# Row maxima of two heads by one VectorE instruction over two PSUM banks, in an attention and feed-forward kernel

## The chip, the cores and the metric

The kernel runs on one core of a Trainium2 chip. The metric is the device time of one execution in microseconds. TensorE (PE, with its weight loads PEld) multiplies matrices, VectorE (DVE), ScalarE (ACT) and GpSimd (POOL) do the work between products, and SyncE (SP) issues nearly all DMAs from one queue. Every engine works through its own list of instructions in order and waits on semaphores for the others. PSUM, where products are accumulated, is used here in banks of 512 fp32 columns on 128 partitions.

## The reference

The reference is attention over four batches and eight heads, with 576 positions of 64 values, followed by two feed-forward layers over the 2304 tokens. The mask lets a position see its own block of 64 and all earlier blocks.

```python
scores = scale * np.matmul(q, k.transpose(0, 1, 3, 2))
mask = block_i >= block_j
scores = np.where(mask, scores, -1000000000.0)
scores = scores - np.max(scores, axis=-1, keepdims=True)
attn = np.exp(scores)
attn = attn / (np.sum(attn, axis=-1, keepdims=True) + 1e-09)
out = np.matmul(attn, v)
...
h = x @ w_in
g = h * np.tanh(sp)
x = g @ w_out
...
h = np.maximum(x @ w_in, 0.0)
return h * h @ w_out
```

`sp` is log(1 + exp(h)). The first `x` is the attention's output with the heads side by side, 2304 x 512; `w_in` is 512 x 2048 and `w_out` 2048 x 512 in both layers. All is fp32, so the scores, the attention's second product and the feed-forward products are made in fp16 pieces (a high and a low part of each factor, three products instead of one), or in fp32 in a few places.

## The kernel before

The work is cut into pieces of 384 tokens, six for each layer. Attention fills the input tile `x` of a first-layer piece, two heads at a time. Two functions do it.

- `attention_lo` (from L1035) takes the 192 earliest queries of a batch for two heads, 16 units in all, in fp32. Its inputs come by two DMAs: q and k packed as 128 x 640 (L1042, into slots named `qk` or `vs`, two instructions of 320 columns in the trace) and v (L1043, `pb`). L1054 makes the scores of both heads in one PSUM bank, L1055 adds the mask, L1059 and L1060 take maxima, L1061 makes the exponent's bias of them, ScalarE takes exponentials, L1067 and L1069 make reciprocals, L823 and L825 scale by them, L1077 to L1080 transpose on PE, and L1092 and L1093 make the second product.
- `attention_hi` takes the other 384 queries of a batch for two heads, 16 units, in split fp16. Each unit has three tiles of 128 queries: tiles 2 and 3 with 320 and 448 keys, and tile 4 with 576, of which the last 128 are made together with tile 2 and the first 448 by themselves. So a unit has three groups of scores (320 + 128, 448 and 448 columns): `scores` (L909, mask at L913) writes head 0 into one PSUM bank and head 1 into the other; the slot for both is called `ab`, and there is only one. `peak` (L922) takes the row maxima, one VectorE instruction for each head. In the first group two copies (recorded at L791 on ScalarE and L793 on VectorE) move the 128 columns of tile 4, one copy for each head, to the SBUF tile `tl`, whose maxima L975 takes. `low` (L927) makes the exponents' bias of the maxima, `expo` (L933) the exponentials on ScalarE, one for each head, `finish` (L943 to L954) the reciprocals and the scaled probabilities as a high part (L953 on ScalarE or L954 on VectorE) and a low part (L818 on VectorE, tile `pb`), which a DMA transposes. `second` (L1018) makes the product with v.

A group of scores therefore holds both banks until the last reader of each is done: the maxima, the copies and the exponentials.

The feed-forward products have several forms: L1352 with an activation at L1357 behind it (PSUM slot `hp`, first half of a layer), L1464 (second half, slot `acc`), and forms with seven products instead of eight, L1385 (first half) and L1503 (second half). Weights of the first layer come raw by L1139 (128 x 8190 bytes each) into `arena` or `pad`, and are made into two fp16 parts by VectorE: a cast (L1149, or on ScalarE) and a shift-and-or (L1150). Later passes read them back from DRAM, where they were spilled (`wspill`). Scaled inputs of a piece go through L1121 (ACT) and L818 (DVE, tile `g`).

Nothing in the code's loops sets the order of the work. Every step is put into a list of tasks by `sch.add`, with engine, cost, tiles read and written; `choose` and `copy` allow a task several engines. The string `PLAN` then gives a position and an engine for each task, and `planned` reads it:

```python
seq = [self.tasks[i + int.from_bytes(raw[2 * i:2 * i + 2], "little", signed=True)] for i in range(n)]
for i, t in enumerate(seq):
    name = ("PE", "ACT", "DVE", "POOL", "SP")[raw[2 * n + i]]
    t.start, t.fillers = float(i), None
    t.eng, t.dur, t.fn, t.lock = [o for o in t.opts if o[0] == name][0] if t.opts else t.first
```

So each engine's list is written out by hand of a table, and semaphores follow from the tiles. A task's `banks` says which of the two PSUM banks it reads, for a rule of the planner that keeps two engines out of one bank at a time. SP's queue takes DMAs in the order of the table too.

Of the kernel before, what the change touches and what calls it, by code (L numbers as in the profile page):

```python
# [68 lines left out]
def seg_len(tiles):  # L69
# [34 lines left out]
    ";%|0Ul6|_5RWHeL^qr0^BRJ(Jxlgw1vwDHvFT>G%pZ3K^dvpV9Ht20Klr@`msN5{uSoJwNZPpv4uUxHz<r%q77V1@UtNg21qxTcoxKdZ?3cX&wl~=IwRe2q`"
    "FS4q>T*2!La<^QD|1Oo;dJ?|6T?WaAaw#$BB30yZX(dm{bX}ki<JpCp1D3|<IQfxJKj;8?LE6bZSldEo>O}ojTg!O;T|0w>CuFStq7CFrovc4<Q|T>l$!Ge#"
    "*2TK}rG`w@Q940C)P7i4Q$EnUh|feUxm||o=Q;*oca}HsSY!EEn<MKLb(Xy<BlI2_qP68c^dGKY>Ye!W9q{u98g)aHf%xSOWdDLTqqT$d!nfB+Wuy86$Uj@|"
    "CE~fJ2k5$-b%*u8#NZNg;W6T{Pan}2vHJ$e0Ac&Jqud9sddfh32qfLD2jl>|d&pxT_L!{KR&oh`Ze|LIOdlDb*MpyX^g3-|dP{p*C%g4VEx@MLa=G@=m2$Oo"
    "*DbnC_SxQgNV{oQyt+Yq>U_!Jc}z3S0O`O<?Q|CV`^gq<t8=w2R^2Wa>NFW99mt+p`28lb;dAtCCS#?o_LBd}Tyo}GITN3@)PL~ujnYF}Xm1%uwiIDu6a7S9"
    "<*&o~2`C#v9{<2&nvNoVAIf}PA#ck-d0!@J8&FqSXMr7&cccZ#pRVKd4R$w?Ux~nIusxLhZ^~<?sZ5lQ^m!T2l^4xI`<6b7?Du(n9{pzMP%!zKJPPI>1Dh}F"
    "2gG%Zenv)?<Fu#sBORv0<Vj9?TOTL#uY=r_JdEwX+M)WO%(JyY%WI%_fc#gU(`q24KX+f$XXGifRi8v|F<Ee>Tx|02=5W0XX=~8^0qR;$PJUd5lIsu2BhrQQ"  # L110
    "9+G}kz9sl$lRipTEx^0|xw8%ruhjv1HNO2<`-A6pWYm3n7r30Jcj!RybhqBh?v~)brQAt{nT>aQfzKKG08wg$$7hnm`@!Yq+DU%Wp2YtSa<RX*lMBhUV{)^O"
    ")SKmYG~1vT>cya^vtFTZ>$Ti(qrKSGNM1#^Q)PjkPHh~?s&mEVTq7#z#YD1`oG0gl>QkhhZpNQA&AG(?9O};5c(5&3+mf|y<#at0UC-7$GP;#C*GAO0#?pt1"
    "IEXtpp>+f5PdRy#E5&&6bYfe`)u!?vEhW`JXCpkgl*~H?+4pKc?)BHxB%4pCQqw=gXCuKt6}f^MogyF4BnPamiMH0ZK-)TS&R{;*qMjbLzfyT$lR{gSx?WGq"
    "NL^T=A_&+H4{X!&GTJ-=+8-iUGl|Lrl4r}~y(84-dt|M>mwP#~#@;PuL2F;UcQ**?2lw;^XXVM!JBY1Nb)J&~+Xss-MD|TcI);p6$n8ay7+@YDL$=_pRb+a9"
    "BJvKXDzHna(PQm);xU~po~HBk4%w;Q&}|11*+EslN!~Tvz)gF0PjH^L)j`YuV1oI&#7?2=EwY<*67^s`o}54g*XrMPjdrDGt|oV8+V*f$C;3a;Qv>TFr#YyZ"
    "58u?{Qx|zaenI1Eaxr<>Le8gV=Tn{9%XgeLi)c?k=QG){9u{mxmYgH4<qPy(NyY9Cc50B5lhJsxj-_T*qDB^=?YC6lue2e49H|{_H#wWUtcSNhqu!own^QZ_"
    "Al`X;AB;6Z*OII6>%aOEIu6r|=o%Uj`)qdAk!Oi<8FUj6w-sx9V&zb3r4s+=K*n1AT`CfRhIlpyPp<&CkAZ=c$+Wuc{EseVZF_Xv&igj7XvnX>i2GP@b4<UH"
    "Hppm56)r=@ucDeC&`rmC>w82wm-^61-jzD!rotn0i0BsBvk3m~j`W)Nye7UWP1YZz+H|I(??r<Pq_RAX?SrtP5KrWj?`5cxkD%!W?Aed4v$SbYoebHfGw4<f"
    "`53^a4S2oXYyKhLIS6OXhw<0Iyz_WpK;F**5!>*6iX9f)en+SIuuQ37D@>n>2YSG%ztBCbq#mtO$ELsO74%dWakY>~9yMSSJXc5s8Vhpr@a=jkZ)x=0Ps9uL"
    "N)vF#biA_zdpA)d_S1>|q?enycz=UV(FNuZQGbb!?P6B$#(ys2%XA(5n-A(vmUB7dU+_Gcm><^)W<9!(=W!A%=ju1`O$VfvHv-~TYszGsVz@EHV^&I=Nm#rI"  # L120
    ">|~e``mKt|FoCh~>^S`sZv9ECm~!wzv3#mWBsAsBA^f{ZvP~T`p1L#G6iKE@(F1PPEVENq;;F#Q)BUndie<A@GY^^t_-2#Lqbr#MpB{uUH_2bJU$V?hdWK~("
    "gPOS$`Ku%_D`hV73eaq+Y?W)wG&;KP&|?Fd{(;ONVP|?B_-hr&%HzBl<j#2fzDuUDqmx-E+vO*DM)%2LnJxby_ct_Kjoi_?P1bXD8K>XJ{>73nf6$H8H*5Ix"
    "EzCQRbGDF8UsEgB%2c^W*UJW3g?4LXh0K(-eBLU1<wyAn8}`W*`je@!(L$`5f)BovTlo7ua;!))%m(a#8*Z2>Z|XcwU5AFhNkw?<Wte6@9dLiWNIyo$YjrSe"
    "dxdU6<MEvJly)auzNK=lm09R{RDPA$(Psrc$t!dRQ{`oHY7u&TCg<p<`1W72^;Y<JGHc$DyYwk+TrOK|A9P!R4U6P=YTyle2A#n5$o_{tJ?Rj7(u15!23|=9"
    "O^~y+hyE!)NNaskuF+On3*K#^6FFxxD_$TIm(pEd1~1H%N%R^`(En-fW$LN=3%>bWN@+(uU58+4GaUm@wbPSyl2q4o=y5)QDc+OA_Diy+wZ1Fg$QN`XHR!6F"
    "Yh4{JRp75zBt)xGRQm=he9Gml(=>~-KOkEh==*ZLJZ8tjEDzec)Qk^gf&Cg8ufRdowTY?D`UlMrWW6gL`5fqTbh;mi+A8$&Z_x3)EEVW(GUzPI(d`_x=fE1m"
    "3H$6SJ6K9%`IYd+Qri!fIb`qR%ANEVeO;eG&+)Dp-EE(d<8}bn6x-*e$kw3i&D1=5j6HewX*poG(QUUd1$KoUXfNaQT3d$B<VN|;mXiJUDLT5Fkd|jvZ<IUb"
    "B(vMjvo}b-onvnyGBblbyM=vy<WJdXH`*RxJkMsDN%nf)Q!r#VnQG5M&n`0EuC(9TE9G6Di)<(9DnGJnp&f_B#_|O#7u$|9#*ViOY-_rTdG>2ooyDpS-0jQ+"
    "@Uv|vKiQdfx;=wxJ>9mE5ABDxx!h~pa?hR9oQ`{rOtTH(?dPe|%~*e$Obw>kW-^6S#<6D-SMCnZkO}q_m}CH1RhMet7g>*SWrY2PDBUXmvDIXl9S*OKvZHJr"
    "sU>gNN<2qX-$&UjB0JQMux07X-={Np&%Qw=t^~il#I-<%*j)PcH_-e!{8&*2S;MtbOcXitUmNliRt>g;@%A8_Wgo=*MRXqb*{AGLD(|awH09+<yNBNG0y~6>"  # L130
    ";6Z!8E!5l~Hz?M7t($2p2bsZMEfd^j``QZ9%I;@6Zeb5lZJXO&FmthSwY$*l<hhE9y_P=eFkM3#`0R-Gu+4+zy4S4M)-cL0bD{kg#_4Js1j}Hx&UOWSmaiMk"
    "c3o}qkW($#Z074Glh5q1+04@Q<~-S8{?IjM35>j!6E35Atv2&ym052VQ)5r3%U^1m$#hd>7U&AIOwS91Y+DRhE-<srbe(S|Q|%|2Ii{xktbd!o={0^}!kWk0"
    "A9aUmO#ida{AGTIkFsR7`Bhh$PsqOC%oO->nVFyy%ui-4fBj(QnI-J`-uzFeQ0;SMjQNtgGtDqFQHPnY`1FZRGtW_DMSkYq%hcGX>B<Y)Ga5Ud!{a0MO?)wu"
    "diNHu|KsiiGfc-L^IP+>x{2UP^SXX)#_F~7Dl?cBN18Eagn7V>(htmVW`}#tDD%F)Z{E^=<}&(^_u+#lnYZ54x6Na8Ag`Kt^m%<)dz)98{w^^?wT)TMvn$=p"
    "VPr4jZbxQ`$Kl9#sJ?yZwg>7n=4(2GvzQLs(C=JiE;4WG!)VmijMfLuVC`a_hjj<i72mDrnP-vli9Vxunk+Mjv!2yk&6#GPwlp`JG1xqW>EJd~)4WE%bPGGL"
# [1763 lines left out]
```

## Time and profile before

| | us |
|---|---|
| median of three runs | 864.63 |
| lowest and highest | 863.62, 864.86 |
| the profiled execution, device time | 863.41 |
| its span | 861.6 |
| PE busy | 845.8 |
| DVE busy | 759.8 |
| ACT busy | 614.9 |
| POOL busy | 63.2 |

The span runs from the first to the last instruction on an engine; the device time of the same execution has 1.8 us more around it. Busy time of an engine counts instructions at work, not waits on semaphores. A row of the timeline gives start, length, engine, line, operation and tiles, with the idle time just before in brackets and what ended it. A row of the groups by line gives the count, the total busy time, and the mean in ns of one instruction. DVE's and ACT's instructions overlap a little at their ends, so two behind each other take less than twice one.

### The profile page before, as it was taken

The numbers are of one execution on the slowest core, as the hardware profiler recorded it, in microseconds if no ns is written. First come the engines' busy times: TensorE is split into PE (matmuls) and PEld (weight loads), VectorE is DVE, ScalarE is ACT, GpSimd is POOL, SyncE is SP. The second block draws the span as 40 slices with busy tenths as digits, with TensorE's granted clock in tenths as the row PEclk, the third lists the DMA queues.
The fourth block names the chain that finished last, engine by engine and source line by source line (L and its number), as shares of the span: only waits on it lengthen the run. The fifth ranks groups of instructions, "written<-read, shape, count | busy, mean of one in ns | idle before, by whom it ended". The sixth has DMA issues, their size and how long they took to land.

```text
span 861.6 us, 19020 instructions
## 1 busy us (share of the span) xinstructions
PE 845.8 (98%) x7233; PEld 606.5 (70%) x7233; DVE 759.8 (88%) x1836; ACT 614.9 (71%) x1224; POOL 63.2 (7%) x70
## 2 busy tenths in 40 slices
...
GB/s 340 382 330 221 208 247 223 279 312 284 260 286 221 258 231 226 246 247 285 272 302 273 306 260 263 269 253 227 209 220 291 225 190 212 258 244 252 186 214 73
DMA packets 163931, 217.24 MB, mean 252 GB/s; under 512 B 107520, under 2 KB 125952, under 8 KB 163840
## 3 DMA queue, kind: packets, MB, share of 16 engines
...
q8 instruction: 56, 0.92, 0.4%
...
HBM read 160.95 MB, written 29.88 MB: 221 GB/s over the span
## 4 chain that ended last, share of the span: by engine, by line
PE 73%; ACT 6%; DVE 5%; DMA 4%; issue 1%; SPq 0%; ACTq 0%; DVEq 0%
PE acc L1464 28%; PE hp L1385 23%; PE hp L1352 10%; PE acc L1503 5%; PE bank L1018 3%; PE bank L909 2%; PE bank L1503 2%; DMA wspill<-arena 1%; DMA arena<-wspill 1%; ACT pad L933 1%; DVE st L922 1%; DVE arena L818 1%; DMA pt<-pb 1%; ACT h L1357 1%; DVE pb L818 1%
## 5 line engine op out<-in xcount | busy, mean ns | idle before, releaser
L1464 PE MATMUL acc<-g,arena 128*128 128x384 f16 x1560 | 301.5, 326 | 0.7 <-DMA arena<-wspill 0.7
L1464 PEld LDWEIGHTS <-arena 128*128 128x128 f16 x1560 | 147.1, 98 | 83.8 <-issue 3.4
L1385 PEld LDWEIGHTS <-arena 128*128 128x128 f16 x1194 | 101.1, 98 | 15.2 <-issue 1.5
L1352 PE MATMUL hp<-xt,first 128*128 128x384 f16 x528 | 102.7, 326 | 1.9 <-ACT h L1357 1.8
L818 DVE SCALAR_TENSOR_TENSOR g<-h,cst,g 128x768 f16<-128x768 f32 x72 | 73.7, 1024 | 6.9 <-ACT g L1121 4.0
L1352 PEld LDWEIGHTS <-first 128*128 128x128 f16 x528 | 49.5, 98 | 42.0 <-issue 10.9
L1385 PEld LDWEIGHTS <-first 128*128 128x128 f16 x816 | 69.5, 98 | 7.4 <-issue 0.5
L818 DVE SCALAR_TENSOR_TENSOR pb<-pad,st,pb 128x384 f16<-128x384 f32 (+2 forms) x96 | 71.6, 754 | 2.8 <-ACT pb L953 2.5
L933 ACT ACTIVATE pad<-bank,st,sq 128x448 f32<-128x448 f32 (+1 forms) x96 | 65.0, 680 | 12.6 <-DVE sv L839 4.9
L1352 PE MATMUL hp<-xt,arena 128*128 128x384 f16 x384 | 73.8, 326 | 0.0
L1385 PE MATMUL hp<-arena 128*128 128x192 f16 x660 | 67.3, 246 | 0.0
L953 ACT ACTIVATE pb<-pad,st 128x384 f16<-128x384 f32 (+2 forms) x81 | 57.1, 716 | 5.5 <-DVE st L945 2.5
L1406 ACT ACTIVATE h<-h,cst 128x576 f32<-128x576 f32 x40 | 30.9, 772 | 35.9 <-DVE h L1404 35.8
L922 DVE TENSOR_REDUCE st<-bank 128x1 f32<-128x448 f32 (+1 forms) x96 | 51.9, 570 | 3.0 <-PE bank L909 2.2
L1385 PE MATMUL hp<-xt,arena 128*128 128x192 f16 x534 | 54.1, 246 | 0.0
L1352 PEld LDWEIGHTS <-arena 128*128 128x128 f16 x384 | 36.2, 98 | 24.0 <-issue 0.8
L1385 PE MATMUL hp<-arena,first 128*128 128x192 f16 x480 | 50.4, 246 | 0.0
L1357 ACT ACTIVATE h<-hp,cst 128x384 f32<-128x384 f32 x76 | 41.8, 577 | 10.9 <-PE hp L1352 9.3
L1402 ACT ACTIVATE h<-hp,cst 128x192 f32<-128x192 f32 x40 | 16.6, 414 | 40.0 <-PE hp L1385 27.1
L1121 ACT ACTIVATE g<-h,cst 128x768 f16<-128x768 f32 x37 | 34.4, 930 | 13.5 <-PE acc L1464 9.2
L1210 DVE TENSOR_TENSOR arena<-arena 128x256 f32<-128x256 f32 x96 | 40.1, 418 | 0.8
L1503 PEld LDWEIGHTS <-arena 128*128 128x128 f16 x504 | 37.5, 98 | 0.0
...
## 6 DMA issues: line engine op xcount, KB each, us to landing
...
```

Of the source, the lines that this page charges most:

```text
L818: return sch.add("DVE", c_dve(n) + 62 * ap, lambda: nc.vector.scalar_tensor_tensor(dst(), a(), s() if ap else s, c(), op0, op1), r=r, w=w, ...
L922: t = sch.add("DVE", c_dve(o1 - o0), lambda hd=hd: nc.vector.reduce_max(st.t[:, 2 * j + hd:2 * j + hd + 1], pp.t[hd][:, o0:o1], axis=AX.X) ...
L933: t = sch.add("ACT", c_act(o1 - o0, True, 3), lambda hd=hd: nc.scalar.activation(pf[hd].t[r0:, k0:k0 + o1 - o0], view(hd)[r0:, o0:o1], AF. ...
L953: "ACT": ("ACT", c_act(n, False, 1), lambda pb=pb, pv=pv, s=s: nc.scalar.activation(pb.t[:, 0:i + 1, 0, :], pv(), AF.Copy, scale=s()), False),
L1121: "ACT": ("ACT", c_act(n, False, 1), lambda: nc.scalar.activation(dst(0), src(), AF.Copy, scale=s()), False),
L1210: plus(ENG["ts"], 256, lambda e, o=o, x=x, y=y, op=op: e.tensor_tensor(b(o), b(x), b(y), op), [], [q])
L1352: nc.tensor.matmul(out=hp.t[:, 0:n], lhsT=w.t[:, f % 2, a, 128 * k:128 * k + 128], rhs=x.t[:, c, k, 0:n], start=k == 0 and i == 0, stop=k ...
L1357: sch.add("ACT", c_act(n, True, 1), lambda f=f, o=o, hp=hp: nc.scalar.activation(h.t[:, o * n:o * n + n], hp.t[:, 0:n], (AF.Mish, AF.Relu) ...
L1385: nc.tensor.matmul(out=bank.t[:, o:o + z], lhsT=lhs, rhs=x.t[:, c, ks[k], :], start=start and k == 0 and i == 0, stop=k == 1 and i == 2, s ...
L1406: sch.add("ACT", c_act(3 * z, False, 1), lambda: nc.scalar.activation(h.t[:, z:2 * n], h.t[:, z:2 * n], fn, scale=hs()), r=[(cst, (HS, j)) ...
L1464: nc.tensor.matmul(out=acc.t[:, 0:n], lhsT=wo.t[:, f % 2, a, 128 * m:128 * m + 128], rhs=g.t[:, c, f % 2 * n:f % 2 * n + n], start=f == 0 ...
L1503: nc.tensor.matmul(out=acc[bank].t[:, o:o + c1 - c0], lhsT=lhs, rhs=g.t[:, c, z * b + c0:z * b + c1], start=j == 0 and (bank, o) in first ...
```

## The change

Four things change, and all lines behind them move up by four at most (L1042 becomes L1038, L1054 becomes L1050, L1139 becomes L1135, L922 becomes L921).

1. The two PSUM tiles `bank0` and `bank1` become halves of one tile `banks` with 1024 columns, and `pairs` is a view of it with the head as an axis.
2. `peak` issues one reduction over `pairs`, both heads' columns, where it issued two; it writes two values per partition.
3. The two copies of the last 128 columns become one of 2 x 128.
4. `PLAN` is another string, so the order on every engine, and the engine of some tasks, is new.

```diff
-    bank = [psp.tile([128, 512], F32, tag=f"bank{i}", name=f"bank{i}") for i in range(2)]
+    banks = psp.tile([128, 1024], F32, tag="bank", name="bank")
+    bank = [banks[:, 512 * i:512 * i + 512] for i in range(2)]
+    pairs = banks.rearrange("p (h c) -> p h c", h=2)
...
         def peak(st, j, pp, o0, o1):
-            for hd in range(2):
-                t = sch.add("DVE", c_dve(o1 - o0), lambda hd=hd: nc.vector.reduce_max(st.t[:, 2 * j + hd:2 * j + hd + 1], pp.t[hd][:, o0:o1], axis=AX.X),
-                            w=[(pp, hd), (st, (j, hd))])
-                t.banks = (hd,)
+            sch.add("DVE", 70.0 + c_dve(2 * (o1 - o0)), lambda: nc.vector.reduce_max(both(st, j), pairs[:, :, o0:o1], axis=AX.X),
+                    w=[(pp, 0), (pp, 1), (st, (j, 0)), (st, (j, 1))]).banks = (0, 1)
...
             if i == 2:
-                for hd in range(2):
-                    t = copy(ENG["tail"], 128, lambda hd=hd: tail.t[:, hd], lambda pp=pp, n=n, hd=hd: pp.t[hd][:, n:n + 128], [], [(pp, hd), (tail, hd)], True)
-                    t.banks = (hd,)
+                copy(ENG["tail"], 256, lambda: tail.t, lambda n=n: pairs[:, :, n:n + 128], [], [(pp, 0), (pp, 1), (tail, 0), (tail, 1)], True).banks = (0, 1)
```

VectorE's list has 96 maxima at L922 before and 48 at L921 after. Of the 32 copies to `tl` 12 were VectorE's and 20 ScalarE's; all 16 new ones are ScalarE's. PE's list has the same 7233 products before and after, in another order in places.

The start of SyncE's queue before. `qk` and `vs` with 128 x 640 are q and k of units of `attention_lo`, `pb` their v, `arena` raw weights.

```order
L1042 DMA qk<-in_qk_dram 128x640 x2
L1042 DMA vs<-in_qk_dram 128x640 x2
L1139 DMA arena<-in_w_dram 128x4095
L1043 DMA pb<-in_vd_dram 128x256
L1042 DMA vs<-in_qk_dram 128x640 x2
L1043 DMA pb<-in_vd_dram 128x256
L1139 DMA arena<-in_w_dram 128x4095
```

The same place in the changed kernel.

```order
L1038 DMA qk<-in_qk_dram 128x640 x2
L1038 DMA vs<-in_qk_dram 128x640 x3
L1039 DMA pb<-in_vd_dram 128x256
L1038 DMA vs<-in_qk_dram 128x640
L1135 DMA arena<-in_w_dram 128x4095
L1039 DMA pb<-in_vd_dram 128x256
L1135 DMA arena<-in_w_dram 128x4095
```

The fifth and sixth blocks of q and k now stand ahead of the first weight, which stood behind the fourth.

VectorE's list near its start, before. `acc_0_177` holds the scores of the third unit, `arena` the first raw weight.

```order
L1061 TENSOR_SCALAR st_182<-st_182 128x3
L768 COPY ident<-ident 128x64
L1149 CAST pad<-arena 128x1024
L1059 TENSOR_REDUCE st_202<-acc_0_177 128x2
L1060 TENSOR_REDUCE st_202<-acc_0_177 128x1
```

The cast's place in the changed kernel; `hp_124` holds the scores of the fifth unit.

```order
L1055 TENSOR_REDUCE st_221<-hp_124 128x2
L825 TENSOR_SCALAR pt<-pt,st_183 128x64
L1057 TENSOR_SCALAR st_211<-st_211 128x3
L1056 TENSOR_REDUCE st_221<-hp_124 128x1
L825 TENSOR_SCALAR pt<-pt,st_183 128x192
L1145 CAST pad<-arena 128x1024
```

The cast of the first weight stood ahead of the maxima of the third unit, and now stands behind those of the fifth.

VectorE's list around one first group of `attention_hi`, the one whose copies stand at 148.47 us in the trace, before. `bank_126` is head 1, `bank_125` head 0.

```order
L922 TENSOR_REDUCE st_1602<-bank_126 128x1
L922 TENSOR_REDUCE st_1602<-bank_125 128x1
L927 TENSOR_SCALAR st_1602<-st_1602,sq_1509 128x2
L818 SCALAR_TENSOR_TENSOR g_1600<-h_1502,cst_1106,g_1600 128x768
L818 SCALAR_TENSOR_TENSOR pb<-pad,st_1390,pb 128x4x128
```

And in the changed kernel.

```order
L921 TENSOR_REDUCE st_1593<-bank 128x2
L925 TENSOR_SCALAR st_1593<-st_1593,sq_1506 128x2
L818 SCALAR_TENSOR_TENSOR g_1585<-h_1497,cst_1093,g_1585 128x768
L818 SCALAR_TENSOR_TENSOR pb<-pad,st_1386,pb 128x4x128
L971 TENSOR_REDUCE st_1623<-tl_1604 128x2
```

ScalarE's list at the same place, before.

```order
L953 ACTIVATE pb<-pad,st_1390 128x4x128
L953 ACTIVATE pb<-pad,st_1382 128x5x128
L791 ACTIVATE tl_1609<-bank_126 128x128
L791 ACTIVATE tl_1609<-bank_125 128x128
L933 ACTIVATE pad,st_1602<-bank_125,st_1602,sq_1509 128x320
L933 ACTIVATE pad,st_1602<-bank_126,st_1602,sq_1509 128x320
```

And in the changed kernel.

```order
L951 ACTIVATE pb<-pad,st_1386 128x4x128
L1117 ACTIVATE g_1585<-h_1497,cst_1093 128x768
L951 ACTIVATE pb<-pad,st_1379 128x5x128
L791 ACTIVATE tl_1604<-bank 128x256
L931 ACTIVATE pad,st_1593<-bank,st_1593,sq_1506 128x320 x2
```

On VectorE one maximum stands where two stood, and what follows is nearly the same. On ScalarE one copy stands where two stood, and it now needs both heads' banks.

## Rows read from the trace of the kernel before

**Rows 1.** The page's first part: the span, and each engine's busy time.

```profile
span 861.6 us, 19020 instructions
PE 845.8 (98%) x7233; PEld 606.5 (70%) x7233; DVE 759.8 (88%) x1836; ACT 614.9 (71%) x1224; POOL 63.2 (7%) x70
```

**Rows 2.** Busy time by stretch: PE, PEld, DVE, ACT, POOL; granted clock, DMA share, GB/s.

```profile
0.00:21.50 21.50, 15.80 (x104) 14.01 (x105) 13.79 (x62) 14.12 (x58) 1.94 (x11) 1.00 0.92 340
21.50:64.60 43.10, 41.94 (x237) 27.52 (x236) 41.11 (x116) 41.73 (x108) 0.00 (x0) 1.00 0.96 356
64.60:344.60 280.00, 276.27 (x1901) 160.83 (x1900) 260.68 (x645) 252.67 (x500) 32.99 (x34) 1.00 0.89 251
344.60:581.60 237.00, 236.99 (x2112) 165.69 (x2110) 227.61 (x555) 195.52 (x384) 14.10 (x14) 1.00 1.03 270
581.60:840.10 258.50, 258.48 (x2674) 222.35 (x2673) 202.27 (x436) 106.23 (x171) 12.80 (x10) 1.00 0.65 227
840.10:861.60 21.50, 16.32 (x216) 16.09 (x213) 14.32 (x27) 4.65 (x7) 1.39 (x1) 0.98 0.22 74
```

**Rows 3.** Waits of PE and ACT: us in total, times, longest.

```profile
PE acc L1054 <- DMA qk<-in_qk_dram: 3.7, 1, 3.7
PE hp L1054 <- DMA vs<-in_qk_dram: 1.8, 1, 1.8
PE hp L1352 <- ACT h L1357: 1.8, 4, 0.9
PE acc L1464 <- DMA arena<-wspill: 0.7, 2, 0.4
...
ACT tl L791 <- DVE st L922: 4.4, 4, 1.4
```

**Rows 4.** Timeline of PE from 9 to 13 us.

```profile
9.13 0.22 PE L1055 MATMUL hp<-small,above 128*128 128x128 bf16 x1
11.15 1.08 PE L1054 MATMUL hp<-vs 128*128 128x192 f32 x6 [1.79 <-DMA vs<-in_qk_dram]
...
12.12 0.28 PE L1077 MATMUL acc<-ident,pt 128*128 128x128 f32 x1
```

**Rows 5.** Timeline of SyncE and DVE in the first 14 us.

```profile
1.67 0.90 SPq L1042 DMA_DIRECT2D vs<-in_qk_dram  x2
2.61 0.43 SPq L1139 DMA_DIRECT2D arena<-in_w_dram  x1
...
3.56 1.00 SPq L1042 DMA_DIRECT2D vs<-in_qk_dram  x2
...
9.96 0.75 DVE L1149 CAST pad<-arena 128x1024 f16<-128x1024 bf16 x1 [1.12 <-DMA arena<-in_w_dram]
...
12.77 1.22 DVE L1150 SCALAR_TENSOR_TENSOR first<-arena,pad 128x1024 uint32<-128x1024 uint32 x1
```

**Rows 6.** Groups by line and shape on DVE and ACT: count, busy us, mean ns, idle before.

```profile
L922 DVE TENSOR_REDUCE st<-bank 128x1 f32<-128x448 f32 x64 | 37.3, 614 | 3.0 <-PE bank L909 2.2 <-PE bank L913 0.6
L922 DVE TENSOR_REDUCE st<-bank 128x1 f32<-128x320 f32 x32 | 14.6, 481 | 0.0
L975 DVE TENSOR_REDUCE st<-tl 128x2 f32<-128x256 f32 x16 | 6.6, 409 | 0.1
L793 DVE COPY tl<-bank 128x128 f32<-128x128 f32 x12 | 3.3, 276 | 0.0
...
L791 ACT ACTIVATE tl<-bank 128x128 f32<-128x128 f32 x20 | 5.2, 266 | 4.4 <-DVE st L922 4.4
```

**Rows 7.** Timeline of DVE at 157 us: a pair of maxima.

```profile
157.82 1.15 DVE L922 TENSOR_REDUCE st<-bank 128x1 f32<-128x448 f32 x2
```

**Rows 8.** Timeline of DVE, ACT and PE between 147 and 158 us.

```profile
147.84 0.88 DVE L922 TENSOR_REDUCE st<-bank 128x1 f32<-128x320 f32 x2
...
148.47 0.56 ACT L791 ACTIVATE tl<-bank 128x128 f32<-128x128 f32 x2
...
157.71 1.14 PE L1352 MATMUL hp<-xt,first 128*128 128x384 f16 x6 [0.92 <-ACT h L1357]
```

More of the change, by code (lines that the diff above doesn't have):

```diff
@@ L104 @@
[L104 to L135, printed above, removed]
@@ new lines @@
+    "?AJ$i1TmVeRpotruu~t9cjYI!Pkz>?VxQkDZxfk2WJv7s_jH%$>F0WrJd5}K)$aO&T#qi#5tXG_*H8Y{r{!i@hOdUmUph)IBSyWYznm)H>l{`*D1GEVa=%<D"
+    "Cvg97y<CRNpSn<o%6uItAIKb?t38OpEPYh|&~DOJ9+ZX18Y!LS7c{@0i2tqA@zPKFANfds&@*K@5vU-)>uumnWQP8tQ`mi){15wE$hGo=4w7lu{k`@Di(|22"
+    "Dt4U%B0s?Im&+GATt@3fGEq+?axJiEypGiC@%ShDs#Zb!5A|%hN?y|XGJ?JDqVJvT?hO)#gXI76Xe2iwc`xXCRd3fPkbFMgt_iwEpzY{*zhHHBb6AHFn=|AN"
+    "e6vAwO|d?vFXP*%z|V#9us)A|*YZ9`&XZw!jqK37b*T1{TlG$|qpf*VH}TlR**iJAjXa3mJ!Bh^y;lq5B)riV9B<dFbOZS4L$(y^&176%vmFdyrOQEW5A7w@"
@@ new lines @@
+    "%o4eTT<N3Tc-~Ju4(d7DTmO{vLGxL}yc1aJptIywqS}tQx04&?e4WYjN9l}?KjDRbJf;ziPoyvS`&t(0mC_d9wbhi2m0lpLpL_-$>&r#bQfKN*c&S)Nv-du1"
+    "{7t9n2eMqI>of9{Oa(8G%P6Aw4rply@+RpFqB2@ab%u73ljT(zCNF^XnKD(r)7Qz$C(Km+fZd<V2s||nJbtdvOFel<_u5C~W3E0eHRNkMLLZX%<XN)!6C{t8"
+    "=kzX4S}2d}TVUmOd0j^7)#i1*k)02+>t$_5yhiFmTcnd%`yV;1&rq92=!bTo3?*~=Aa{_wNtO(d_p~>)?E$#}i!YHE^&#T4A35FSF7UORY`916#jj83-7;La"
+    ">g}NK4q2?X63O%N?gO0ASI@<J_kfh!s4sc?px(jbMma<7B^TS02{&thd6a9XlCg%!UQ4FT(UW*SroZYTH0r{mp1EBAPi`lst<k2JTtWQrq#m3g=Mt-d)Wy--"
@@ new lines @@
+    "kJk(E=lRkKea|P~*2o*$o>k4!qm_v1F8Oj1)%rrNH9%@_Jx`hv`ObO{x;K>WdK&n6SvzW7IZK*>`mXr(KAxvjeP2c6$MqCF1wCHT7s$fXLFUccQa>XCB2R(q"
+    "je3H%1a&#m6y1ucL@i{s45E%1);6W;HKD@Zr#I<wat~J5!smBsW2#XlPN=A}z|u}m7dcZaXf1O63@uOAyd-s{r?$~Zvs7&jd4d&#siIlr_7E^$iRvSqx1U_S"
+    "A1%u9yhC0y|DhUJl-ks_n`NMUFZtHh!&^arjyxmJliw-!4du-1sIvojXNX6MuF;zMhyBYAA;S;o!(`e%BD|K2+O3z7eLKm~TS5QzW(V=Qk!pEA)vcRsp^DDe"
+    "`Pv0`o5yQ6@^TA)dD(2CrgemszM@Lx+ci2Fmia+{#N(UvJEA{Nd%}r%dV#Fq?ku9T3KT7XQ5M?csFS5SPFLw*DpW_9=^LcXB>!3x#pybV)zgu7wp53w<`T^_"
@@ new lines @@
+    "(QT6sv@OWv4(vD$Mr}vEPD=;g_aI-sqgvEM&KRoY1@a2gi;3KPIHNPMuS|v>OQv*WWm~f66Ha&>Np0nQJsIEDAv<2>HIMx*sj0=_;aK@Ee7R5GAO=fxpe~X{"
+    ";y5Ww8sNJuIR&}xr44$uM8Z(LA50FVzCA|fH-nQOWnUBd5$`?>D>lH=e>IZ3LF!k;W<Gwj;HV>*m?&paeP$7lGda657BwJ?2f)qy(5|R#F(@o7+liD>#J3fk"
+    "aXDwsBO)X5&PIJ%8WGhV>dyETbajCfzqQM$*UP}?lX5n-ZxQvp5>b4ddR{<}P^9Z%<aKCtKRn-tOwXgz)#ChL(Cb6Ax(6PrjAcK-_?9YKOc!vgG>6$Dxdn_Y"
+    "qkH%hBnq;(QEC6x*+||7M;svE|HQuj=>IL)n@wHYf#-Hp0k&glA$7GtztEpR!(uSLC4P*-=5h2}tKpXR?A!?#7qWLHUJ+y-Vr4t(Q3+ht-t0r}-_+7(<o8z2"
@@ new lines @@
+    "+W{}`1C5)|VG5^wZBBxdC&68-;g3A6ZgNazInLBDf546vO#^ISsTP0bnrt%(R%~yU(@p)z)p1z(Jxp98WArui4S$Q_h;4FErszQ`**v<QNvg6(${};NtmP4z"
+    "HJty5DPUj9lrwvzR33!Q%IIts>3Z0Dp*Awba;MphCzt99St>h-UPH51mho<eY>|Itt4!8w%~F|9ZkLF{AOCW%SpKH=&F1XY`XM$?lwGnxme8T?#vj}09SV8="
+    "EGuLI8So{$mq>Z@oy?JqGEeS=(Pn}D`SPoLL0&C_MV88EbWrQ$OFlI-`Sg;9Wu-JW8<BZ6eZ@$fEDg;<R;=Qr*>aoKHOt7DNit5SlLt%WQ+#s}Zu$kCpVTqr"
+    "&qwgxpE6k{$y>1DB2NFDTKR^i&0jKsYWo{JGmrJV*!#L(t-sU7jU{@M^c%TRzoM_omp|aYYxH9M1*A_Vn|_y>@_)Ko9@BAD_aCL4euCZ)vHBvtjjr)|8KQr|"
```

132 lines of the change are left out of this document (71 added, 61 removed).

## The prediction

> **What bounds the kernel now.** I read the page first, then a table by stretches, then TensorE's waits, and only then the lines that the diff touches. The page's first part [rows 1] gives PE 98% of an 861.6 us span: 845.8 us busy, so 15.8 us idle in all. The table [rows 2] says where those lie: 5.70 us in the first 21.5 us, 1.16 us from 21.5 to 64.6, 3.73 us from 64.6 to 344.6, 0.01 us from there to 581.6, 0.02 us from there to 840.1, and 5.18 us behind 840.1. The granted clock is 1.00 in all but the last stretch (0.98 there), so TensorE ran at its 2.4 GHz level and has nothing to win from the clock. A stretch without idle time can give nothing back to a lighter VectorE. All the time to be had from faster attention work therefore lies before 344.6 us, at most 5.70 + 1.16 + 3.73 = 10.6 us, and 3.7 of it is the wait for the very first input, which the new order leaves first in its queue.
>
> Who ends those idle times is in the waits [rows 3]: once 1.8 us for the fifth block of q and k at the start, 1.8 us in four places for the activation behind `hp`, 0.7 us for weight DMAs. None of these names the maxima. VectorE is busy 260.68 of 280.00 us (93%) between 64.6 and 344.6 and ScalarE 252.67 (90%) [rows 2], so the maxima matter there only through the queue they stand in.
>
> **The 48 merged maxima.** Before, 96 instructions: 64 over 448 columns at 614 ns and 32 over 320 at 481 ns [rows 6]. That is (614 - 481) / 128 = 1.04 ns a column and 614 - 448 x 1.04 = 148 ns that do not depend on the columns. But the fixed part is not all paid when two stand behind each other: a pair of 448 takes 1.15 us from the first start to the last end [rows 7], so the second starts 1.15 - 0.61 = 0.54 us after the first, 0.08 us before that one ends. A pair costs the queue 2 x 0.54 = 1.08 us. One instruction over 2 x 448 columns should last 0.148 + 896 x 0.00104 = 1.08 us and hold the queue 0.08 us less, 1.00 us. Rounded up from the two widths I take 0.07 us saved by each, 48 x 0.07 = 3.4 us of VectorE. No row shows an instruction that reads two banks. The end on one side is that the whole fixed part goes, 48 x 0.148 = 7.1 us; on the other that the change of bank costs it a second time inside the instruction, which makes it 0.08 us dearer than the pair, 3.7 us lost. I stay near the middle because the maximum over the SBUF tile `tl` reads two runs of 128 at 409 ns [rows 6], and 148 + 256 x 1.04 = 414: a second run cost nothing there.
>
> The Trainium skill, page "Perfetto Trace Analysis", section "Optimizing Scalar/DVE Operations", puts the overhead of a VectorE instruction on PSUM at about 125 ns of engine time. By that the estimate would be 48 x 0.125 = 6.0 us instead of 3.4, and the total below 0.3 us lower. The pair in rows 7 shows 0.07, and I keep that.
>
> **The 16 merged copies.** Before, 12 copies of 128 columns ran on VectorE at 276 ns and 20 on ScalarE at 266 ns [rows 6]. In the new order all 16 are on ScalarE. VectorE loses 12 x 0.276 = 3.3 us. ScalarE had 20 x 0.266 = 5.3 us; one copy of 256 columns lies between 0.27 us (as one) and 0.53 us (as two); the middle, 0.40, makes 6.4 us, 1.1 us more. Together VectorE is lighter by 6.7 us, ScalarE heavier by about 1 us. From 344.6 us on this is worth nothing, since PE has no idle time there that it could fill.
>
> Between 64.6 and 344.6 PE idles 3.73 us, and 1.8 of that is the wait for the activation on ScalarE [rows 3], in front of which a load of a function table and exponentials stand; it is one instance of 0.92 us at 157.71 [rows 8] and three smaller ones. ScalarE gets no lighter. Of the other 1.9 us I take two fifths, **0.8 us**, as what a lighter VectorE gives; ends 0 and 3.7.
>
> **What the order moves at the start.** This is the larger term. SyncE issued four blocks (to 2.57 us), then a weight at 2.61, then the fifth block at 3.56 [rows 5]. PE finished the fourth score group at about 9.3 us and waited 1.79 us for the fifth block [rows 4]; it then ran the first transposes at 12.12. In the new order the fifth block stands directly behind the fourth, in front of the weight. A weight is 128 x 8190 bytes, 1.05 MB; with the 0.13 MB of `pb` that is 1.18 MB less ahead of it, at 340 GB/s [rows 2] 3.5 us. So it would land at about 11.15 - 3.5 = 7.7 us, before PE is free for it at 9.3: the wait goes. On VectorE the cast of the first weight stood in front of the third unit's maxima, and waited 1.12 us for its DMA [rows 5] while those scores were ready; in the new list it stands behind the maxima of five units. Ends: 0, if what follows does not keep up, and 1.79. From 21.5 to 64.6 us ScalarE is busy 41.73 of 43.10 and VectorE 41.11 [rows 2], so not all of it will be kept; I take two thirds, **1.2 us**.
>
> PE's own list has the same instructions in other places, no more of them; POOL has one fewer. The end of the program (the last products, then the sums and four stores) keeps its chain: one evacuation goes from ScalarE to VectorE, both idle there.
>
> **The sum** against the profiled execution's own 863.41 us: 863.41 - 1.2 - 0.8 = 861.4. That execution lies 1.22 us under the median of the three runs, 864.63, so for a median I forecast 864.63 - 2.0 = **862.6 us**.
>
> **Rivals.** One: the same. The fifth block comes early but the units behind it are held by ScalarE, and VectorE's 6.7 us lie under PE. For it: 97% busy ScalarE in the second stretch, PE waits that name ScalarE and DMAs. Against: the 1.79 us hole is a plain DMA wait with a plain cause. Time: 864.63 less a few tenths, 864.3.
>
> Two: slower, because the weights become late. The order that lets the attention blocks ahead pushes the weights back: the first by 0.79 MB in SyncE's list (two blocks and one `pb`), later ones by up to 0.6 MB. At the 356 GB/s of the second stretch 0.6 MB is 1.7 us, and the DMA engines are busy 0.92 to 0.96 of these stretches [rows 2], so it isn't made up. A weight that lands late must then pass a cast of 0.75 us and a shift-and-or of 1.22 us [rows 5] on a VectorE that is 95% busy: up to 2.0 us more. Half of that gives 1.7 + 1.0 = 2.7 us and 867.3 us. It decides only once a product with a raw weight waits for VectorE or a weight DMA between 33 and 64 us, and no row of the present waits shows that there.
>
> Three: slower, because one instruction holds both banks. ScalarE could copy head 0's columns at 148.47 while VectorE still read head 1's bank, its pair of maxima running from 147.84 to 148.72 [rows 8]; now the copy must wait for the whole. At that place it is little: the two copies ended at 149.03, the merged one would end at 148.72 + 0.40 = 149.12. But ScalarE's copies already waited 4.4 us in four places for the maxima [rows 3]. If each of these grew by one maximum, 4 x 0.54 = 2.2 us, with the activations for PE behind them and no gain at the start, it would be 866.8 us. The Trainium skill, same page and section, says that where an engine isn't saturated but causes bubbles on others, breaking instructions up may let work be completed sooner: it speaks against merging. The place at 148 us gives it 0.1 us, the four waits more.
>
> Four: a larger gain. The whole 1.79 us and 3.0 of the 3.73 us go: 864.63 - 4.8 = 859.8 us.
>
> **How the numbers follow.** A measurement of this kernel can tell about 0.2% from no change, 1.7 us, so faster means below 862.9 and slower above 866.4. Forecast (862.6) 0.42, larger gain (859.8) 0.08, the same (864.3) 0.32, late weights (867.3) 0.12, both banks held (866.8) 0.06. So faster 0.50, same 0.32, slower 0.18. The two ends of the maxima's price (7.1 us saved, 3.7 us lost) lie mostly under PE and move the total by less than 1 us. The forecast's own range is 861.0 to 863.7. For eight in ten I go to 859.6 below, which takes in the larger gain, and to 866.4 above, which leaves out most of the two slower cases.
>
> **What would show it.** Right: the fifth score group without an idle time before it, and the first transposes near 10.5 instead of 12.12 us; 48 maxima of about 1.08 us (448) and 0.81 us (320); PE idle under 4.2 us in the first 21.5 us and near 2.9 us from 64.6 to 344.6; PE busy time unchanged. Wrong in the start: PE idle moves to waits on the casts or on weight DMAs before 64 us. Wrong in the price: merged maxima of 1.15 us and more. Wrong in the cover: an idle time of PE after 344.6 us, where none stands now, which would be the work of the order, not of the two merged instructions.

## The result: slower by 1.4%, and the profile after

The changed kernel takes 876.21 us (median of 5 runs, 873.30 to 877.09) beside 863.62 us for the kernel before (5 runs). The ratio is 1.0142 with a 95% interval from 1.0124 to 1.0160. The forecast was 862.6 us and a range that ended at 866.4. The profiled execution of the change took 873.3 us, the fastest of its five.

The page's first part, for the change. It answers to [rows 1].

```profile
span 871.5 us, 18920 instructions
...
PE 849.0 (97%) x7233; PEld 607.0 (70%) x7233; DVE 758.0 (87%) x1779; ACT 616.8 (71%) x1221; POOL 61.6 (7%) x69
```

VectorE is 1.8 us lighter and ScalarE 1.9 us heavier, and the span is 9.9 us longer. TensorE idles 871.5 - 849.0 = 22.5 us where it idled 15.8, and is busy for 3.2 us more with the same 7233 products. The busy time may hold a part of the waits. The 1560 products at L1460 last 326 ns each by their records and count 299.2 us together, 192 ns each, as they overlap in a flow; a product behind a break in the flow would count more of its length. How much of the 3.2 us that is the profile doesn't tell.

Busy time by stretch, for the change, with the same columns and bounds as [rows 2] up to 840.1 us.

```profile
0.00:21.50 21.50, 17.08 (x111) 15.52 (x112) 14.74 (x67) 15.02 (x60) 1.94 (x11) 1.00 0.94 348
21.50:64.60 43.10, 37.99 (x203) 23.62 (x202) 35.97 (x98) 36.48 (x101) 1.53 (x1) 1.00 0.86 311
64.60:344.60 280.00, 275.99 (x1902) 160.92 (x1901) 262.33 (x628) 251.60 (x496) 23.86 (x27) 1.00 0.90 254
344.60:581.60 237.00, 233.75 (x2041) 161.00 (x2039) 224.46 (x523) 196.09 (x381) 17.25 (x16) 1.00 0.99 264
```

In the first stretch TensorE's idle time fell from 5.70 to 4.42 us. In the second it rose from 1.16 to 5.11 us, and there VectorE, ScalarE and the DMA engines are less busy too: none of them sets the pace, all of them wait. From 64.6 to 344.6 us it is 4.01 us where it was 3.73. From 344.6 to 581.6 us, where there was no idle time, there are 3.25 us.

TensorE's waits in the change (us in total, times, longest), to be held against [rows 3].

```profile
PE acc L1050 <- DMA qk<-in_qk_dram: 4.4, 2, 3.7
PE bank L1161 <- DVE st L1055: 1.4, 1, 1.4
PE bank L837 <- ACT pad L931: 1.2, 2, 0.6
PE bank L1161 <- ACT pt L1060: 1.1, 2, 0.7
...
PE bank L1161 <- ACT pad L931: 0.9, 1, 0.9
...
PE bank L1161 <- ACT pt L791: 0.6, 1, 0.6
PE bank L1161 <- DVE st L1056: 0.5, 1, 0.5
```

L1161 is a product with one to four output columns for the weights' norms, into columns from 448 on of bank 1 (L1165 before). Its inputs come from ScalarE's squares at L1158, yet here it waits for maxima (L1055, L1056), exponentials (L1060, L931) and a copy (L791). These read scores or transposes. The products' groups by line:

```profile
L1161 PE MATMUL bank<-us,onesq 128*128 128x1 bf16 x24 | 4.0, 166 | 4.3 <-DVE st L1055 1.4 <-ACT pt L1060 1.1 <-ACT pad L931 0.9
L837 PE MATMUL bank<-sv,ones 128*128 128x1 bf16 x16 | 2.7, 168 | 1.2 <-ACT pad L931 1.2
```

Before, the same two groups:

```profile
L1165 PE MATMUL bank<-us,onesq 128*128 128x1 bf16 x24 | 4.0, 167 | 0.2 <-ACT wsq L1162 0.2
...
L837 PE MATMUL bank<-sv,ones 128*128 128x1 bf16 x16 | 2.7, 167 | 0.0
```

4.3 us of idle time for 24 products that take 0.17 us each, where 0.2 us stood. The longest one in the timeline of the change (TensorE and VectorE):

```profile
49.93 0.22 PE L1051 MATMUL bank<-small,above 128*128 128x128 bf16 x1
49.98 0.86 PE L1426 MATMUL acc<-h,late 128*128 128x384 f32 x2
...
50.52 1.22 DVE L1146 SCALAR_TENSOR_TENSOR late<-arena,pad 128x1024 uint32<-128x1024 uint32 x1
...
51.66 0.55 DVE L1055 TENSOR_REDUCE st<-bank 128x2 f32<-128x384 f32 x1
...
52.26 0.16 PE L1161 MATMUL bank<-us,onesq 128*128 128x1 bf16 x1 [1.41 <-DVE st L1055]
```

The maximum at 51.66 stands behind a shift-and-or of 1.22 us in VectorE's queue, and TensorE waits for it with every product behind L1161. In TensorE's list of the change this place reads, with the semaphores that each row waits for:

```
L1051 MATMUL bank<-small,above 128x128
L1426 MATMUL acc_1_591<-h_521,late 128x384
L1161 LDWEIGHTS onesq
L1161 MATMUL bank<-us_571,onesq 128x1 [waits DVE_49]
```

With two tiles and all else in the same order (the first experiment) the same rows read:

```
L1058 MATMUL bank_125<-small,above 128x128
L1433 MATMUL acc_1_592<-h_522,late 128x384
L1168 LDWEIGHTS onesq
L1168 MATMUL bank_126<-us_572,onesq 128x1 [waits Activation_49]
```

The scores lie in `bank_125`, bank 0; the small product goes to `bank_126`, bank 1. As one tile, the two are ordered against each other, so the small product waits for the maximum of scores in the other bank. As two tiles it waits for ScalarE alone. The count that it waits for there is reached, behind the square of its own inputs, by an exponential (L1067 there, L1060 of the change) that reads bank 1, its own bank.

### The profile page after: what moved, and what is told of

The parts are those of the page before. It is cut to its first block, busy times and chain, and to the rows that moved or that the text cites. A ratio compares the mean times of both kernels' runs of the same rounds, so it can differ in the third digit from the quotient of the medians.

```text
span 871.5 us, 18920 instructions
## 1 busy us (share of the span) xinstructions
PE 849.0 (97%) x7233; PEld 607.0 (70%) x7233; DVE 758.0 (87%) x1779; ACT 616.8 (71%) x1221; POOL 61.6 (7%) x69
## 4 chain that ended last, share of the span: by engine, by line
PE 80%; ACT 8%; DVE 7%; DMA 3%; issue 1%; SPq 0%; DVEq 0%; ACTq 0%
PE acc L1460 28%; PE hp L1381 20%; PE hp L1348 13%; PE acc L1499 4%; PE acc L1426 3%; PE bank L909 3%; PE bank L1014 2%; PE bank L1499 2%; ACT pad L931 1%; DMA arena<-wspill 1%; DMA qk<-in_qk_dram 1%; PE bank L1050 1%; DVE st L921 1%; ACT wsq L1158 1%; DVE pb L818 1%
## 5 line engine op out<-in xcount | busy, mean ns | idle before, releaser
L1460 PE MATMUL acc<-g,arena 128*128 128x384 f16 x1560 | 299.2, 326 | 1.7 <-DVE g L818 1.0
L1460 PEld LDWEIGHTS <-arena 128*128 128x128 f16 x1560 | 146.5, 98 | 87.4 <-issue 8.6
L1381 PEld LDWEIGHTS <-arena 128*128 128x128 f16 x1194 | 101.3, 98 | 15.9 <-DMA arena<-wspill 1.4
L1348 PE MATMUL hp<-xt,arena 128*128 128x384 f16 x384 | 72.0, 326 | 0.0
L931 ACT ACTIVATE pad<-bank,st,sq 128x448 f32<-128x448 f32 (+1 forms) x96 | 65.1, 681 | 5.6 <-DVE st L925 2.3
L951 ACT ACTIVATE pb<-pad,st 128x640 f16<-128x640 f32 (+2 forms) x76 | 53.8, 720 | 7.4 <-DMA late<-pb 3.6
L1348 PEld LDWEIGHTS <-arena 128*128 128x128 f16 x384 | 36.0, 98 | 24.1 <-issue 1.2
L921 DVE TENSOR_REDUCE st<-bank 128x2 f32<-128x896 f32 (+1 forms) x48 | 47.8, 995 | 3.3 <-PE bank L909 1.3
L1400 DVE TENSOR_TENSOR h<-first,hp 128x384 f32<-128x384 f32 x40 | 22.0, 550 | 18.8 <-PE hp L1381 18.3
L1117 ACT ACTIVATE g<-h,cst 128x768 f16<-128x768 f32 x39 | 36.2, 929 | 2.6 <-DVE h L1365 1.4
```

The lines of the kernel that those rows point to most:

```text
L921: sch.add("DVE", 70.0 + c_dve(2 * (o1 - o0)), lambda: nc.vector.reduce_max(both(st, j), pairs[:, :, o0:o1], axis=AX.X), w=[(pp, 0), (pp, 1 ...
L931: t = sch.add("ACT", c_act(o1 - o0, True, 3), lambda hd=hd: nc.scalar.activation(pf[hd].t[r0:, k0:k0 + o1 - o0], view(hd)[r0:, o0:o1], AF. ...
L951: "ACT": ("ACT", c_act(n, False, 1), lambda pb=pb, pv=pv, s=s: nc.scalar.activation(pb.t[:, 0:i + 1, 0, :], pv(), AF.Copy, scale=s()), False),
L1117: "ACT": ("ACT", c_act(n, False, 1), lambda: nc.scalar.activation(dst(0), src(), AF.Copy, scale=s()), False),
L1348: nc.tensor.matmul(out=hp.t[:, 0:n], lhsT=w.t[:, f % 2, a, 128 * k:128 * k + 128], rhs=x.t[:, c, k, 0:n], start=k == 0 and i == 0, stop=k ...
L1381: nc.tensor.matmul(out=bank.t[:, o:o + z], lhsT=lhs, rhs=x.t[:, c, ks[k], :], start=start and k == 0 and i == 0, stop=k == 1 and i == 2, s ...
```

## The experiments

Theory A says that the one tile, by such waits, is the whole loss. Theory B puts it down to the new order, theory C to the merged instructions that hold both banks. Each run is compared with the kernel before on the same chip; its medians there were 863.09, 863.79 and 864.00 us.

**New order, two tiles, two maxima and two copies** (`a_two_pairs`). Against the change:

```diff
-    banks = psp.tile([128, 1024], F32, tag="bank", name="bank")
+    bank = [psp.tile([128, 512], F32, tag=f"bank{i}", name=f"bank{i}") for i in range(2)]
...
+            def maxima():
+                for hd in range(2):
+                    nc.vector.reduce_max(st.t[:, 2 * j + hd:2 * j + hd + 1], pp.t[hd][:, o0:o1], axis=AX.X)
```

> The new order kept, but two PSUM tiles again and two maxima and two copies where the change has one of each. Theory A (the one tile of two banks makes instructions wait for readers and writers of the other bank, or of other columns): these waits are gone, so 861 to 866 us, and the idle time of TensorE before the one-column products (L1161 of the change, 4.3 us there) falls under 1.5 us. Theory B (the new order itself is late somewhere): stays at 872 to 877 us. Theory C (one instruction that holds both banks): 861 to 866 us as under A, so this run does not tell A from C.

Measured: 862.42 us, ratio 0.9992 (0.9975 to 1.0008). Before the 24 small products TensorE idles 0.1 us in all, where it idled 4.3 us in the change. The order alone costs nothing, and theory B falls.

**New order, one tile, two maxima and two copies** (`a_one_pairs`). Against the run before it:

```diff
-    bank = [psp.tile([128, 512], F32, tag=f"bank{i}", name=f"bank{i}") for i in range(2)]
+    banks = psp.tile([128, 1024], F32, tag="bank", name="bank")
+    bank = [banks[:, 512 * i:512 * i + 512] for i in range(2)]
...
```

> The new order and the one tile of two banks kept, but two maxima and two copies. Theory A: as slow as the change or slower by the 48 more maxima, 873 to 879 us, with the same idle time before the one-column products (4 us or more). Theory B: 872 to 877 us. Theory C: the cost goes with the merged instructions, 862 to 867 us.

Measured: 876.76 us, ratio 1.0178 (1.0160 to 1.0195). Without any merged instruction it is as slow as the change, TensorE idles 4.7 us before the same 24 products, and theory C falls too.

**Old order, one tile** (`b_one`), against the kernel before:

```diff
-    bank = [psp.tile([128, 512], F32, tag=f"bank{i}", name=f"bank{i}") for i in range(2)]
+    banks = psp.tile([128, 1024], F32, tag="bank", name="bank")
+    bank = [banks[:, 512 * i:512 * i + 512] for i in range(2)]
...
```

The line left out names a view of the tile that nothing in this run uses.

> The kernel before, its order and its two maxima and two copies, with nothing changed but the two PSUM tiles made halves of one. Theory A: slower by 5 to 13 us, 869 to 877 us, with new idle time of TensorE that is ended by engines which read the other bank. Theories B and C: no difference, 862 to 865 us.

Measured: 877.41 us, ratio 1.0181 (1.0160 to 1.0201), a little above the range expected. No instruction, order or engine differs from the kernel before, only how PSUM is declared. TensorE's waits in it name readers of either bank (L1167 is the weights' small product there, L886 another one in the same spare columns, L911 the scores, L935 the exponentials):

```profile
PE bank L886 <- DVE sq L832: 1.5, 2, 1.0
PE bank L1167 <- ACT pad L935: 1.3, 2, 0.9
PE bank L911 <- ACT pad L935: 1.2, 2, 0.9
...
PE bank L1167 <- ACT pt L793: 0.7, 1, 0.7
```

**Old order, one tile, one maximum** (`b_one_max`). The first of the two tasks of a group does nothing, the second issues the merged reduction:

```diff
+            seen = []
             for hd in range(2):
-                t = sch.add("DVE", c_dve(o1 - o0), lambda hd=hd: nc.vector.reduce_max(st.t[:, 2 * j + hd:2 * j + hd + 1], pp.t[hd][:, o0:o1], axis=AX.X),
+                t = sch.add("DVE", c_dve(o1 - o0), lambda: seen.append(1) if not seen else nc.vector.reduce_max(both(st, j), pairs[:, :, o0:o1], axis=AX.X),
```

> As the run before it (old order, one tile), and the two maxima of a group made one instruction at the later one's place. Theory A: within 2 us of that run, since the maxima themselves are 0.08 us a pair cheaper or nothing. Theory C: slower than that run by 3 us or more. Merged maxima of 1.08 us over 2 x 448 columns and 0.81 us over 2 x 320, as in the change.

Measured: 876.76 us, ratio 1.0164 (1.0150 to 1.0178), 0.65 us from the run before it: the merged maxima add none of the 3 us that theory C asks for.

**The change without waits for the other bank** (`a_free`). Instructions, order and the one tile are those of the change. Every instruction on the tile waits only for those of other engines that use a bank it uses itself (`used` and `mine` are the sets of banks of an earlier instruction and of this one):

```diff
+            keep = [(o, mybir.DependencyReason.DATA) for o, used in reversed(log[-400:]) if used & mine]
+            for e in {o.engine for o, _ in log} - {inst.engine}:
+                tc.declare_no_dep(inst, group=f"banks {e}", keep=[o for o, _ in keep if o.engine == e], reason="other bank")
...
+                    tc.add_manual_dep(inst, o.name, info[why], reason="same bank")
...
             t.fn()
+            apart(t)
```

> The change as it is (new order, one tile, one maximum and one copy for both heads), but each instruction on the tile waits only for those that use the same bank; the waits for the other bank are declared away. Theory A (the waits across the two banks are the whole loss): 860 to 863.5 us, at or a little under the run with two tiles and the new order (862.42), since the merged maxima make VectorE 3 us lighter under TensorE. Theory C (a merged instruction that holds both banks costs by itself): 865 us or more. Should part of the loss stand elsewhere (the 48 + 16 merged instructions, the engine they stand on), 866 to 872 us.

Measured: 860.80 us (12 runs, 859.66 to 862.59), ratio 0.9965 (0.9952 to 0.9977): faster than the kernel before, and 15.4 us faster than the change. Its page and its groups:

```profile
span 858.1 us, 18935 instructions
...
PE 846.2 (99%) x7233; PEld 607.0 (71%) x7233; DVE 757.6 (88%) x1779; ACT 615.2 (72%) x1221; POOL 61.7 (7%) x69
```

```profile
L1161 PE MATMUL bank<-us,onesq 128*128 128x1 bf16 x24 | 4.0, 167 | 0.1
...
L837 PE MATMUL bank<-sv,ones 128*128 128x1 bf16 x16 | 2.7, 169 | 0.0
```

TensorE's idle time is down to 858.1 - 846.2 = 11.9 us, and its busy time to 846.2, near that of before. The idle time before L1161 went from 4.3 to 0.1 us.

**The same for the first 386 of 4853 tasks alone** (`a_free_start`), against the run before it:

```diff
-            apart(t)
+            if t.start < 386.0:
+                apart(t)
```

> The change as it is, with the waits for the other bank declared away for the first 386 of 4853 tasks alone, some 50 us of TensorE's work (all units of the early queries but four, and the first weights). If the lost time adds up place by place: the early stretch gives back some 6 us of the 15 that a_free gained, 868 to 872 us. If the late start is what makes everything behind it late: 861 to 865 us. If the early waits are made up for later anyway: 874 to 877 us.

Measured: 869.25 us (8 runs, 867.92 to 873.39), ratio 1.0061 (1.0040 to 1.0083), so 7.0 of the 15.4 us. Divided at this one place the loss adds up, and close to half of it stands in the first 50 us of TensorE's work.

**Old order, one tile, no waits for the other bank** (`b_free`), the control: `b_one` with the lines that `a_free` adds.

```diff
             t.fn()
+            apart(t)
```

> The order of before, one tile, two maxima and two copies, waits for the other bank declared away. Theory A: back at the kernel before, 862 to 865 us, where the same with those waits (b_one) took 877.4. If the tile costs by something other than waits, 868 us or more.

Measured: 863.37 us, ratio 0.9994 (0.9974 to 1.0014). The 14 us of `b_one` are these waits, and nothing else of the tile.

**As that, with one maximum** (`b_free_max`): `b_free` with the `peak` of `b_one_max`.

> As b_free, with the two maxima of a group as one instruction. If the merge gains little without the new order (its 3 us of VectorE lie under TensorE): 861.5 to 864.5 us, no difference from before that can be measured. If the 3 us that a_free gained are the merge's by itself: 859.5 to 861.5 us. If one instruction on both banks costs: 865 us or more.

Measured: 865.72 us, ratio 1.0010 (0.9996 to 1.0023). The median missed the range expected and lies in the one named for a cost, but the ratio shows no clear difference from the kernel before; a cost of up to 0.23% is not excluded. Merged maxima alone win nothing in the old order, as the new order alone wins nothing (`a_two_pairs`). Both together win 0.35% (`a_free`).

**Two mixed orders in three runs, which missed** (`hy_330`, `hy_400`, and `hy_330_free` with the merged instructions and without the waits). In `a_two_pairs` TensorE idles only 0.40 us between 21.5 and 344.6 us, then it waits for weights:

```profile
PE hp L1388 <- DMA arena<-wspill: 2.9, 2, 1.5
```

So I took the new order's first part and the old one's rest; only `PLAN` differs. As lists of tasks:

```diff
-order = new
+order = new[:2080] + [t for t in old if t not in new[:2080]]
```

> Two tiles, two maxima and two copies, with the new order for the first 2080 of 4853 tasks (some 330 us of TensorE's work) and the order of before for all others. Theory D (the new order wins about 5 us of TensorE's idle time before 345 us, and its later part gives 3 to 4 us back in waits for spilled weights between 345 and 582 us): 857.5 to 860.5 us, with under 1 us of idle TensorE time from 345 to 582 us. Rival (those waits come of TensorE being earlier, whatever the order): 861.5 to 863.5 us, with the waits for spilled weights still there.

> As the run before it, with the change of order at task 2503 (some 400 us of TensorE's work). Theory D: 857.5 to 860.5 us, within 1 us of that run, as TensorE has no waits in the new order between these two points. Rival: 861.5 to 863.5 us.

> The order of hy_330 with the merged maxima and copies on one tile and no waits across its banks. Theories A and D together: 857 to 860.5 us, faster than the kernel before by 0.3% or more, and within 1 us of hy_330. If the merged instructions cost by themselves: slower than hy_330 by 2 us or more.

Measured: 863.53 us (ratio 0.9995, 0.9981 to 1.0010), 861.92 us (0.9984, 0.9969 to 0.9999) and 862.38 us (0.9987, 0.9969 to 1.0004). Theory D falls for the first: the waits for spilled weights are there in the old order as well once TensorE is earlier, 1.9 us in two places at the same line, at 512.94 and 576.21 us. The second lies in the rival's range, with 1.8 us of such waits, and the third misses the 857 to 860.5 us expected. None of them is faster than `a_free`. The line of `hy_330`:

```profile
PE hp L1388 <- DMA arena<-wspill: 1.9, 2, 1.4
```

## Why the prediction was wrong

The step that failed is the list of the change itself. The prediction costed the maxima, the copies and the order, and gave the first part of the diff, two PSUM tiles made one, no term and no rival. It said that TensorE's list "has the same instructions in other places, no more of them". That is so, and what they wait for is what changed. In the old order this part alone takes 14 us (`b_one` against `b_free`); in the new one 15.4 us (the change against `a_free`).

The other steps, by the numbers that the prediction gave:

- *Maxima of 1.08 and 0.81 us.* Right; the rows of the change, with the copies:

```profile
L921 DVE TENSOR_REDUCE st<-bank 128x2 f32<-128x896 f32 x32 | 34.7, 1085 | 2.8 <-PE bank L909 1.3 <-PE bank L913 0.5 <-PE bank L884 0.5
L921 DVE TENSOR_REDUCE st<-bank 128x2 f32<-128x640 f32 x16 | 13.0, 815 | 0.5 <-PE bank L913 0.5
```

```profile
L791 ACT ACTIVATE tl<-bank 128x256 f32<-128x256 f32 x16 | 6.0, 373 | 3.2 <-DVE st L921 2.8 <-DVE st L938 0.4
```

- The second bank inside one instruction costs nothing that these rows show, and the saving of 3.4 us was sized rightly. With the same order, engines and tile the pairs (`a_one_pairs`, below) take 36.8 + 14.1 = 50.9 us and the merged maxima 34.7 + 13.0 = 47.7 us, 3.2 us less.

```profile
L923 DVE TENSOR_REDUCE st<-bank 128x1 f32<-128x448 f32 x64 | 36.8, 616 | 2.6 <-PE bank L909 1.1 <-PE bank L884 0.5 <-PE bank L913 0.5
L923 DVE TENSOR_REDUCE st<-bank 128x1 f32<-128x320 f32 x32 | 14.1, 481 | 0.5 <-PE bank L913 0.5
```

- VectorE's whole busy time fell by less between these two, from 759.8 to 758.0 us; in the old order it fell by 3.5 us (761.1 in `b_free`, 757.6 in `b_free_max`). The estimate of 6.0 us, by the Trainium skill's page "Perfetto Trace Analysis", section "Optimizing Scalar/DVE Operations", is further off.
- *VectorE lighter by 6.7 us, ScalarE heavier by about 1 us.* Wrong: 1.8 and 1.9 us. The sum took in the maxima and the copies alone, but the new order moves other work to VectorE as well. For example, 13 instead of 10 of the scalings `arena<-arena,us` over 1024 columns are VectorE's (2.2 us more) and 9 instead of 5 of `late<-acc,cst` (2.3 us more).
- *The copy at 0.40 us* measured 0.373, in all 6.0 us where 6.4 were forecast.
- *The start.* The mechanism was right. In the change the fifth group follows the fourth without a gap and the first transposes stand at 11.00 us, where 10.5 was forecast and 12.12 stood [rows 4]:

```profile
8.97 1.04 PE L1050 MATMUL hp<-vs 128*128 128x192 f32 x6
...
9.90 1.04 PE L1050 MATMUL hp<-vs 128*128 128x192 f32 x6
...
11.00 0.30 PE L1073 MATMUL acc<-ident,pt 128*128 128x128 f32 x1
```

The half us behind the forecast is about what TensorE's third group of scores lost: it lasts 1.69 us here and 1.04 us in the executions of the kernel before and of `a_free_start`. The latter, in the same order, has its first transposes at 10.49 us. A wait of 0.70 us for another block of q and k stands at 15.41 us in the change.

- *The terms 1.2 and 0.8 us* were too small, as `a_free` shows, where the other bank's waits are away:

```profile
0.00:21.50 21.50, 17.05 (x105) 15.58 (x106) 14.29 (x66) 14.68 (x59) 1.94 (x11) 1.00 0.92 345
21.50:64.60 43.10, 42.92 (x240) 28.39 (x239) 41.66 (x111) 41.81 (x110) 1.54 (x1) 1.00 0.96 361
64.60:344.60 280.00, 279.72 (x1944) 162.55 (x1943) 266.43 (x635) 255.12 (x511) 27.79 (x30) 1.00 0.91 255
344.60:581.60 237.00, 235.13 (x2086) 164.15 (x2085) 221.31 (x516) 191.59 (x370) 14.81 (x13) 1.00 1.03 268
```

The same stretches with the order alone (`a_two_pairs`):

```profile
0.00:21.50 21.50, 16.87 (x105) 15.41 (x106) 14.25 (x66) 14.78 (x60) 1.94 (x11) 1.00 0.92 343
21.50:64.60 43.10, 43.10 (x241) 28.45 (x240) 41.83 (x111) 41.92 (x110) 1.54 (x1) 1.00 0.97 367
64.60:344.60 280.00, 279.60 (x1943) 162.81 (x1942) 266.94 (x662) 255.63 (x519) 27.01 (x30) 1.00 0.91 254
344.60:581.60 237.00, 233.20 (x2071) 162.73 (x2070) 221.09 (x534) 191.02 (x374) 15.04 (x13) 1.00 1.01 265
```

- Idle time of TensorE in `a_free` against [rows 2]: up to 64.6 us 4.63 instead of 6.86, 2.2 us won; from 64.6 to 344.6 us 0.28 instead of 3.73, 3.5 us won; from there to 581.6 us 1.87 instead of 0.01, 1.9 us given back. The sum, 3.8 us, is near the 3.5 us between the spans (861.6 and 858.1). The forecast had 2.0, the median of `a_free` 3.0 against its own before. So in size the forecast comes near the change without its first part, but partly by luck: both terms were too small, and what is given back had none. The prediction named idle time behind 344.6 us as a sign against its cover, and it came, 3.25 us in the change.
- The term of 0.8 us has the wrong cause. `a_two_pairs` has two maxima for each group, and its VectorE is busier between 64.6 and 344.6 us than that of before (266.94 beside 260.68 us), yet TensorE's idle time is 0.40 us there, and 4.63 us up to 64.6, as in `a_free`. What is won before 344.6 us in these single executions is the order's, not that of a lighter VectorE.
- *The rival of one instruction holding both banks* named the right danger at the wrong place. The copies' wait for the maxima did not grow: 2.8 us in three places, beside 4.4 in four [rows 3].

```profile
ACT tl L791 <- DVE st L921: 2.8, 3, 2.1
```

- *The rival of late weights* is not what happened: no wait of TensorE before 64 us names a weight's cast or its DMA. A weight's shift-and-or only made the wait at 52.26 us longer.

What stays open: why the merge and the order win together (`a_free`) what neither wins alone. By the rows above the two differ behind 344.6 us, where the order alone gives back 3.80 us and `a_free` 1.87. The waits for spilled weights are 3.1 us in `a_two_pairs` and 1.1 us in `a_free`, but nothing was tried that shows why.
